# Pooled attention into a residual MLP on one core: a new order for the first batch, fillers on TensorE, and two transposes moved from DMA to TensorE in the second

## Chip, cores, metric

The kernel runs on one core of one Trainium2 chip. The metric is the time of one execution on the device in microseconds (us); the figure for a kernel is the median of its runs.

## What is computed

For each of 8 batches the reference does attention over 8 heads of 64 channels and 576 positions, with keys and values averaged over groups of 8 positions, so that a head has 72 keys. The heads side by side are the 512 channels of x. Then a mixer over positions and an MLP over channels follow, each with a residual.

```python
k_p = k.reshape(B, H, Sp, pool, D).mean(axis=3)      # pool = 8, Sp = 72; v_p likewise
attn = softmax(scale * np.matmul(q, k_p.transpose(0, 1, 3, 2)))
x = np.matmul(attn, v_p)                             # then (B, S, H * D)
a1 = alpha1 * x + beta1
tok = np.einsum('ts,bsd->btd', w_tok, a1)            # over the 576 positions
u = x + lam * tok
a2 = alpha2 * u + beta2
ch = np.maximum(a2 @ w_ch1, 0.0) @ w_ch2             # 512 -> 2048 -> 512
out = u + lam * ch
```

## The kernel before

Everything that TensorE multiplies is bf16 or fp16; sums are fp32 in PSUM. A batch has four chunks of 128 positions and a rest of 64; the rests of two batches share one chunk, so 8 batches make 36 chunks. Four chunks are one block of the MLP, and there are nine blocks.

**The stages of a batch.** `att_F` brings q to channel-major form (qT), `att_Frem` does so for the rest of 64 positions. `att_K` sums the keys in groups of 8 by a product with `pool_main` and evacuates them to `kpT`. `att_S` makes the scores of a head and ScalarE's exponential of them (ET, L441, two instructions a head). `first_V` (batches 0 and 1) pools the values by TensorE. `att_AV` multiplies by the values, and VectorE divides by the row sum into `x_tm` (L461, L463). `att_X` makes `xs`, the operand of the mixer, from two heads at a time (L470, L474), on VectorE or GpSimd. `mix_T` is the mixer of one chunk: five products (L504), then VectorE adds x (`u_sb`, L506) and scales to bf16 (`u_bf`, L508). `mix_uT` brings `u_bf` to channel-major form (`u_fm`), either by a DMA transpose on SyncE's queue (L518) or by four TensorE transposes (L523) and a ScalarE copy (L525).

**The MLP of a block.** `mlp_A(n, j)` is four products for 128 of the 2048 hidden channels and a ScalarE ReLU into Hj (L544). `mlp_B(n, m, part)` is four of the 16 products of one output chunk m (L557); after part 3, VectorE adds u (L562) and the result is stored. `scale_w2(g)` multiplies a quarter of the second weight by lam on VectorE (L327), once; `mlp_B` of block 0 takes its parts in the order of those quarters.

**What sets the order.** No scheduler moves anything: each engine runs its instructions in the order in which the code issues them, and waits only for semaphores. The first batch (L571 to L642) is written out call by call. From L690 on, each block n gathers a list of calls with a due number ("slot") and issues them sorted by it: `mlp_A` number j has slot j, the sixteen `mlp_B` have slots 16 to 31, and the attention of batch n + 1 is put between them by the numbers in `attention(b)`. Loads of batch n + 2 are in the same list. The numbers only order the calls; they are not times.

**Queues of DMAs.** SyncE issues q's rest, k and v from batch 2 on, the stores and the DMA transposes; GpSimd's queue issues all loads that change type (q, the first k and v, all weights), between its own arithmetic; ScalarE's queue issues the small vectors at the start. A load with `behind` is preceded by a one-column write of the destination on VectorE, so it can't start before VectorE has come to that place.

**Constants.** `broadcast` spreads a row over 128 partitions by an fp32 product with a row of ones (L266) and a ScalarE copy. `more_constants` (L252) makes ones, a zero tile `warm`, the zero rows of `xs` and `wtT`, and two products of one row each (L260). `setup_wtok` transposes the mixer's weight by TensorE, `setup_rowsum` makes its row sums, `setup_bias` the MLP's bias. `keep_warm(count)` (L490) is `count` products of 128 x 512 whose result nothing reads. `gp` (L52) takes one of six PSUM buffers.

Of the kernel before, what the change touches and what calls it, by code (L numbers as in the profile page):

```python
# [14 lines left out]
P = 128  # L15
# [8 lines left out]
def kernel(  # L24
# [102 lines left out]
    def load_v(b, u, parts=(0, 1)):  # L127

        if parts[0] == 0:
            st1[b]["v"][u] = work.tile([SPG, 4, 8, D], FP, tag="v_u", bufs=2, name="v_u")  # L130
        v_u = st1[b]["v"][u]
        for part in parts:
            g0, g1 = ((0, 64), (64, SPG))[part]
            nc.sync.dma_start(
                out=v_u[g0:g1].rearrange("g h p d -> g h (p d)"),
                in_=v[b, 4 * u:4 * u + 4, 8 * g0:8 * g1].rearrange("h (g p) d -> g h (p d)", p=8))
# [57 lines left out]
    load_vector(2, moe_alpha2)  # L194
    nc.scalar.dma_start(out=b2row, in_=moe_beta2.rearrange("(c p) -> c p", p=P))
    identity = const.tile([P, P], FP, tag="identity", name="identity")
# [14 lines left out]
    load_q_bf(0, 1)  # L211
    for t, n, width in ((pool_main, 64, 2),):
        nc.gpsimd.affine_select(out=t, in_=t, compare_op=ALU.is_ge, fill=0.0, base=0,
                                pattern=[[-width, n]], channel_multiplier=1)
        nc.gpsimd.affine_select(out=t, in_=t, compare_op=ALU.is_ge, fill=0.0, base=width - 1,
                                pattern=[[width, n]], channel_multiplier=-1)
# [4 lines left out]
    nc.gpsimd.affine_select(out=identity, in_=identity, compare_op=ALU.not_equal,  # L221
                            fill=1.0, base=0, pattern=[[-1, P]], channel_multiplier=1)
# [11 lines left out]
    for i in range(H):  # L234
# [3 lines left out]
    nc.vector.tensor_reduce(out=pool_rem, in_=pool_each, op=ALU.max, axis=AX.X)  # L238
# [5 lines left out]
                            in1=pool_v[0:32, 1:16:2], op=ALU.add)  # L244

    warm = const.tile([P, DM], BF, tag="warm", name="warm")
    b2c_bf = const.tile([P, 4], BF, tag="b2c_bf", name="b2c_bf")
    xs_pool = [const.tile([P, 5, DM], BF, tag=f"xs_{i}", name=f"xs_{i}") for i in range(2)]
# [3 lines left out]
    def more_constants():  # L252
        nc.vector.memset(ones_bf, 1.0)
        nc.vector.memset(ones_lo[0:64], 1.0)
        nc.vector.memset(ones_lo[64:128], 0.0)
        nc.vector.memset(warm, 0.0)
        nc.vector.memset(xs_pool[1][0:64, 4, :], 0.0)
        nc.vector.memset(wtT[:, :, S:640], 0.0)
        for i, p0 in ((0, 64), (1, 0)):
            nc.vector.tensor_tensor(out=xs_pool[i][p0:p0 + 1, 4, :], in0=vecs[p0:p0 + 1, 3],  # L260
                                    in1=vecs[p0:p0 + 1, 0], op=ALU.mult)
# [80 lines left out]
    def att_F(b, hp, copy=nc.scalar.copy):  # L342


        st = st1[b]
        u, r = hp // 2, hp % 2
        if r == 0:
            st["qT"][u] = work.tile([P, 8, P], BF, tag="qT", bufs=4, name="qT")
        if b:
            if r == 0:  # L350
                nc.sync.dma_start_transpose(out=st["qT"][u],
                                            in_=st["q"][u].rearrange("p h c d -> p (h c d)"))
            return
        ps_q = gp("ps_q").bitcast(BF)
        for c in range(4):
            nc.tensor.transpose(
                out=ps_q[:, 128 * c:128 * c + 128],
                in_=st["q"][u][:, 2 * r + c // 2, 2 * (c % 2):2 * (c % 2) + 2].rearrange(
                    "p c d -> p (c d)"),
                identity=identity_bf)  # L360
        copy(out=st["qT"][u][:, 4 * r:4 * r + 4, :],
                       in_=ps_q[:, 0:512].rearrange("p (c t) -> p c t", c=4))
# [16 lines left out]
    def att_K(b, u, copy):  # L379
# [13 lines left out]
        for hh in range(2):  # L393
            for c in range(nr):
                nc.tensor.matmul(  # L395
                    out=kp[:, hh:4:2, 64:72],
                    lhsT=st["rem"][1][:, hh, c:c + 2].rearrange("p a d -> p (a d)"),
                    rhs=pool_rem.rearrange("p (g u r) -> p u r g", r=2, u=2)[:, u],
                    start=(c == 0), stop=(c == nr - 1))
        for a in range(2):  # L400
# [89 lines left out]
    def keep_warm(count):  # L490

        ps = gp("ps_warm")
        for _ in range(count):
            nc.tensor.matmul(out=ps, lhsT=identity_bf, rhs=warm)
# [16 lines left out]
    def mix_uT(key):  # L511
# [5 lines left out]
        if key[0] > 1 or key in ((1, 0), (1, 1), (0, 4)):  # L517
# [53 lines left out]
    new_batch(1)  # L571
    broadcast(1, lamal_bc)
    broadcast(0, lam_bc)
    att_F(0, 0)
    att_F(0, 1, nc.vector.tensor_copy)
    cast_rem(0, nc.vector)
    att_K(0, 0, None)
    att_Frem(0, nc.scalar.copy)
    att_S(0, 0)
# [3 lines left out]
    att_S(0, 2)  # L583
    att_K(0, 1, None)
    nc.vector.tensor_tensor(out=lamal_bc, in0=lamal_bc, in1=lam_bc, op=ALU.mult)
    more_constants()
    att_S(0, 3)
    att_S(0, 4)
    first_V(0, 0)
    att_AV(0, 0)  # L590
    att_S(0, 5)
    att_AV(0, 1)
    for g in range(4):
        load_w1(g)
    att_X(0, 0, 2, nc.gpsimd)
# [5 lines left out]
    broadcast(2, al2_bc)  # L601
    setup_vectors()
    load_q_bf(1, 0)
    load_q_bf(1, 1)
    att_X(0, 2, 4, nc.gpsimd)
    load_w2(0)
# [3 lines left out]
    att_X(0, 4, 6)  # L610
# [5 lines left out]
    load_rem(1, behind=nc.vector)  # L616
# [4 lines left out]
    att_X(0, 6, 8)  # L621
    mix_T(0, 0, nc.gpsimd)
    setup_rowsum(2)
    setup_rowsum(3)
    mix_T(0, 1, nc.gpsimd)
    load_v16(1)
    for g in range(1, 4):
        load_w2(g)
# [16 lines left out]
    def attention(b):  # L645
# [4 lines left out]
        if first:  # L650
            todo.append((3.3, lambda: att_F(b, 0)))
            todo.append((3.4, lambda: att_F(b, 2)))
            todo.append((3.5, lambda: cast_rem(b, nc.gpsimd)))
            todo.append((6.0, lambda: att_Frem(b)))
# [10 lines left out]
        for u in range(2):  # L665
# [4 lines left out]
            if first:  # L670
                todo.append((10.2 + 1.4 * u, lambda u=u: first_V(b, u, nc.scalar.copy)))
        for h in range(8):
            at = 8.8 + 1.1 * h if first else 7.4 + 1.15 * h
            lag = 3.0 if first else 2.0
# [76 lines left out]
```

## Time and profile before

| what | us |
|---|---|
| median of three runs (lowest, highest) | 370.04 (369.24, 370.18) |
| the profiled execution's own time | 369.66 |
| its span, from the first instruction to the last | 368.0 |
| TensorE, products | 349.7 busy, 95% |
| VectorE | 213.3, 58% |
| ScalarE | 151.5, 41% |
| GpSimd | 89.2, 24% |
| mean granted clock of TensorE | 0.978 of full |

Times in the views count from the start of the span. A row of a timeline gives start, duration, engine, line and operation, what is written and read with its shape, how many instructions are merged, and in brackets the idle time before it and what ended that. A table by stretches gives the busy us of each engine in each stretch, the share of full clock that TensorE was granted, the mean busy share of the 16 DMA engines (over 1 where the packets of one engine overlap) and what they moved. Busy says that an engine had an instruction running, not that it ran at full speed.

### The profile page before, as it was taken

The page shows a single profiled execution, that of the slowest core. Times are in us where ns is not written, and L with a number is a line of the kernel's source. Part 1 is how long each engine was busy: PE and PEld are TensorE (multiplying, and loading weights), DVE is VectorE, ACT ScalarE, POOL GpSimd, SP SyncE. Part 2 cuts the span into 40 slices and gives each one's busy share as a digit, 9 for nine tenths or more (in the row PEclk, how much of TensorE's full clock was granted, in tenths as well). Part 3 has the DMA queues.
Part 4 walks back from the last instruction along what each step waited for, and adds up shares of the span by engine and source line. Part 5 has one row for each costly group of instructions (what it writes and reads, how often), then busy time and mean ns, then how long its engine had stood idle before and what let it go on. Part 6 is the DMA issues. An engine that isn't in the chain of part 4 may idle for free.

```text
span 368.0 us, 5803 instructions
## 1 busy us (share of the span) xinstructions
PE 349.7 (95%) x2161; PEld 190.7 (52%) x2201; DVE 213.3 (58%) x449; ACT 151.5 (41%) x312; POOL 89.2 (24%) x97
## 2 busy tenths in 40 slices
PE   5799899979999999999999999999999999999994
PEld 2566566435654565456545654565446544544542
DVE  5566035898777587658765887587748871011011
ACT  3434588014830483048303830384038403703700
POOL 8353905980004300250044003500330000000000
PEclk9958999999999999999999999999999999999998
DMA  8999994419829763688289728874730032011012
GB/s 127 203 205 256 187 272 93 58 35 235 161 73 219 141 126 68 175 179 159 72 209 145 139 74 207 149 143 83 206 89 0 20 96 71 2 57 57 3 57 57
DMA packets 69232, 45.17 MB, mean 123 GB/s; under 512 B 35850, under 2 KB 60494, under 8 KB 69204
## 3 DMA queue, kind: packets, MB, share of 16 engines
q1 hardware_dynamic: 54112, 34.03, 39.0%
q0 software_dynamic: 15072, 10.76, 19.9%
q8 instruction: 17, 0.28, 0.3%
q14 instruction: 11, 0.09, 0.1%
q10 hardware_dynamic: 20, 0.01, 0.0%
HBM read 38.04 MB, written 9.44 MB: 129 GB/s over the span
## 4 chain that ended last, share of the span: by engine, by line
PE 85%; DVE 6%; DMA 5%; issue 2%; ACT 1%; SPq 1%; DVEq 0%
PE ps_ch L557 32%; PE ps_h L539 31%; PE ps_tok L504 10%; PE ps_sc L436 4%; DMA v_u<-in_v_dram 3%; PE ps_av L455 2%; DMA rem_raw<-in_k_dram 1%; PE ps_sc L439 1%; DVE u_bf L508 1%; PE ps_kp L389 1%; DVE w L327 1%; DVE u_sb L506 1%; DVE x_tm L463 1%; DMA rem_qT<-rem_q 1%; DVE xs L470 1%
## 5 line engine op out<-in xcount | busy, mean ns | idle before, releaser
L544 ACT ACTIVATE Hj<-ps_h,bias_cols 128x512 bf16<-128x512 f32 x144 | 98.8, 688 | 158.6 <-PE ps_h L539 157.7
L539 PE MATMUL ps_h<-u_fm,w 128*128 128x512 bf16 (+2 forms) x572 | 137.1, 374 | 1.1
L557 PE MATMUL ps_ch<-w,Hj 128*128 128x512 bf16 x560 | 132.3, 379 | 0.9
L557 PEld LDWEIGHTS <-Hj 128*128 128x128 bf16 x576 | 55.0, 98 | 62.2
L539 PEld LDWEIGHTS <-w 128*128 128x128 bf16 x592 | 62.5, 114 | 44.8 <-issue 0.8
L562 DVE TENSOR_TENSOR u_sb<-u_sb,ps_ch 128x512 f32<-128x512 f32 x36 | 24.7, 687 | 75.5 <-PE ps_ch L557 75.2
L504 PE MATMUL ps_tok<-xs,wtT 128*128 128x512 bf16 (+1 forms) x197 | 49.5, 380 | 0.7 <-DVE xs L470 0.4
L441 ACT ACTIVATE ET<-ps_sc 72x256 f16<-72x256 f32 (+1 forms) x128 | 44.9, 405 | 6.7 <-PE ps_sc L436 6.3
L506 DVE TENSOR_TENSOR u_sb<-x_tm,ps_tok 128x512 f32<-128x512 f32 (+1 forms) x40 | 27.4, 686 | 26.4 <-PE ps_tok L504 26.4
L142 POOL CAST rem_q<-rem_raw 128x256 bf16<-128x256 f32 x7 | 5.3, 751 | 129.4 <-DMA rem_raw<-in_q_dram 129.3
L463 DVE TENSOR_TENSOR x_tm<-ps_av,rec 128x320 f32<-128x320 f32 x64 | 31.5, 492 | 2.3
L504 PEld LDWEIGHTS <-wtT 128*128 128x128 bf16 (+1 forms) x200 | 19.5, 98 | 24.3 <-issue 1.0
L508 DVE TENSOR_TENSOR u_bf<-u_sb,al_bc 128x512 bf16<-128x512 f32 (+1 forms) x38 | 29.4, 775 | 1.5
L461 DVE RECIPROCAL rec<-ps_av 128x5 f32<-128x5 f32 x64 | 12.3, 192 | 25.7 <-PE ps_av L459 24.8
L424 DVE TENSOR_TENSOR v_u<-v_u 72x512 f32<-72x512 f32 (+1 forms) x48 | 26.5, 553 | 1.2
L436 PE MATMUL ps_sc<-qT,kpT 128*72 128x256 bf16 x128 | 26.4, 288 | 0.7 <-ACT kpT L402 0.4
L455 PEld LDWEIGHTS <-ET 72*128 72x128 f16 x256 | 16.7, 102 | 14.7 <-DVE vp L417 2.9
L155 POOL TENSOR_TENSOR k_raw<-k_raw 128x512 f32<-128x512 f32 x14 | 18.7, 1333 | 14.6 <-DMA k_raw<-in_k_dram 11.3
L455 PE MATMUL ps_av<-vp,ET 72*128 72x66 f16 x256 | 19.1, 199 | 2.6 <-DVE vp L417 2.6
L157 POOL TENSOR_TENSOR k_bf<-k_raw 128x512 bf16<-128x512 f32 x14 | 21.3, 1524 | 1.1
L470 DVE TENSOR_TENSOR xs<-x_tm,lamal_bc 128x512 bf16<-128x512 f32 x27 | 18.7, 692 | 0.9
L402 DVE CAST kpT<-ps_kp 64x288 bf16<-64x288 f32 x26 | 11.8, 455 | 9.4 <-PE ps_kp L395 6.1
(109 smaller groups left out, 214.0 us busy)
## 6 DMA issues: line engine op xcount, KB each, us to landing
out_dram<-u_sb SPq DMA_DIRECT2D x32, 256.0 KB
k_raw<-in_k_dram SPq DMA_DIRECT2D x14, 512.0 KB
v_u<-in_v_dram SPq DMA_DIRECT2D x12, 512.0 KB
q_bf<-in_q_dram POOLq DMA_DIRECT2D x16, 256.0 KB, 5.0
w<-in_moe_w_ch_dram POOLq DMA_DIRECT2D x8, 512.0 KB, 11.1
rem_raw<-in_q_dram SPq DMA_DIRECT2D x16, 64.0 KB
rem_raw<-in_k_dram SPq DMA_DIRECT2D x16, 64.0 KB
v<-in_v_dram POOLq DMA_DIRECT2D x4, 256.0 KB, 6.1
```

The source lines that it names most:

```text
L424: nc.vector.tensor_tensor(out=t[:, :, 0:n], in0=t[:, :, 0:n], in1=t[:, :, n:2 * n], op=ALU.add)
L436: nc.tensor.matmul(out=ps_sc[0:SPG, 0:256], lhsT=kpT_pool[u][:, half, h % 4, :], rhs=st["qT"][u][:, 2 * (h % 4):2 * (h % 4) + 2, :])
L441: nc.scalar.activation(out=ET[:, n0:n0 + n], in_=ps_sc[0:SPG, 0:n], func=AF.Exp, bias=0.0, scale=0.125)
L455: nc.tensor.matmul(out=av[:, c, :], lhsT=ET[:, m0:m0 + 128], rhs=vp1[:, hh, :])
L463: nc.vector.tensor_tensor(out=x[:, :, dd:dd + D], in0=av[:, :, 0:64], in1=rec.unsqueeze(2).to_broadcast((P, 5, D)), op=ALU.mult)
L504: nc.tensor.matmul(out=ps_tok, lhsT=wtT[0:kk, at, t0:t0 + P], rhs=xs[0:kk, sc, :], start=(sc == 0), stop=(sc == 4))
L506: nc.vector.tensor_tensor(out=s["u"][p0:p1, :], in0=st1[b]["x"][p0:p1, c, :], in1=ps_tok[p0:p1, 0:DM], op=ALU.add)
L508: eng.tensor_tensor(out=s["u_bf"][p0:p1, :], in0=s["u"][p0:p1, :], in1=al2_bc[p0:p1, :], op=ALU.mult)
L539: nc.tensor.matmul(out=ps_h[:, t0:t1], lhsT=w1_of(cc, j), rhs=u_fm[n][:, cc, t0:t1], start=(cc == 0), stop=(cc == 3))
L544: nc.scalar.activation(out=t, in_=ps_h, func=AF.Relu, bias=bias_cols[:, j:j + 1], scale=1.0)
L557: nc.tensor.matmul(out=ps, lhsT=Hj[n, j][:, 128 * m:128 * m + 128], rhs=w2[j // 4][:, j % 4, :], start=(j == 0), stop=(j == NJ - 1))
L562: nc.vector.tensor_tensor(out=u, in0=u, in1=ps, op=ALU.add)
```

## The change

Five things are done.

- First batch, constants. `warm` and the zero rows of `xs_pool[1]` are made at the start. The two one-row products move from `more_constants` into `bias_rows`, called behind `cast_rem`. `more_constants`, with what is left of it, is called before the first scores instead of before the fourth. The product of `lamal_bc` and `lam_bc` runs inside the first `att_K`. `identity` is made earlier on GpSimd. `al2_bc` is no longer spread by TensorE: a DMA on SyncE loads it as a broadcast, behind a write of VectorE (`load_al2`). The transposed copy of q's second piece goes from VectorE to ScalarE, and `att_Frem` is before `att_K`.
- Unread products. `keep_warm` takes its PSUM from the pool of `ps_ch` and its weights from `warm`; nine products in seven more calls are put into the first batch.
- Order of loads and of `att_X` in the first batch: `load_w1(2)`, `load_w1(3)` and the four `load_w2` come later, batch 1's q, rest and v earlier, and the third `att_X` goes to GpSimd, so that its queue runs three `att_X` with no load between.
- Second batch. Its q (`att_F`, `att_Frem`) and its chunks 0 and 1 of u (`mix_uT`) are transposed by TensorE and copied by ScalarE, no longer by DMA.
- Slots in block 0: row sum 4 is parted from its transposes, `mix_T(0, 4)`, the scalings of w2, values, mixer and `mix_uT` of batch 1 move. `mix_uT` of chunk 3 goes from 26.8 to 29.1. The loads of batch 2's k, v and rest get a write of VectorE before them.

Core of the diff ("..." where lines are left out):

```diff
-    def load_v(b, u, parts=(0, 1)):
+    def load_v(b, u, parts=(0, 1), behind=None):
...
+        if behind is not None:
+            for rows_ in (slice(0, 64), slice(64, SPG)):
+                behind.memset(v_u[rows_, 0, 0, 0:1], 0.0)
...
-    load_vector(2, moe_alpha2)
...
+    warm = const.tile([P, DM], BF, tag="warm", name="warm")
+    nc.vector.memset(warm, 0.0)
...
+    nc.gpsimd.affine_select(out=identity, in_=identity, compare_op=ALU.not_equal,
+                            fill=1.0, base=0, pattern=[[-1, P]], channel_multiplier=1)
...
-    nc.gpsimd.affine_select(out=identity, in_=identity, compare_op=ALU.not_equal,
-                            fill=1.0, base=0, pattern=[[-1, P]], channel_multiplier=1)
...
-    nc.vector.tensor_reduce(out=pool_rem, in_=pool_each, op=ALU.max, axis=AX.X)
+    xs_pool = [const.tile([P, 5, DM], BF, tag=f"xs_{i}", name=f"xs_{i}") for i in range(2)]
+    nc.vector.memset(xs_pool[1][0:64, 4, :], 0.0)
...
+    nc.vector.tensor_reduce(out=pool_rem, in_=pool_each, op=ALU.max, axis=AX.X)
+
+    def bias_rows():
+        for i, p0 in ((0, 64), (1, 0)):
+            nc.vector.tensor_tensor(out=xs_pool[i][p0:p0 + 1, 4, :], in0=vecs[p0:p0 + 1, 3],
+                                    in1=vecs[p0:p0 + 1, 0], op=ALU.mult)
...
-    warm = const.tile([P, DM], BF, tag="warm", name="warm")
...
-    xs_pool = [const.tile([P, 5, DM], BF, tag=f"xs_{i}", name=f"xs_{i}") for i in range(2)]
...
-        nc.vector.memset(warm, 0.0)
-        nc.vector.memset(xs_pool[1][0:64, 4, :], 0.0)
...
-        for i, p0 in ((0, 64), (1, 0)):
-            nc.vector.tensor_tensor(out=xs_pool[i][p0:p0 + 1, 4, :], in0=vecs[p0:p0 + 1, 3],
-                                    in1=vecs[p0:p0 + 1, 0], op=ALU.mult)
+
+    def load_al2(behind):
+        behind.memset(al2_bc[:, 0:1], 0.0)
+        nc.sync.dma_start(out=al2_bc, in_=moe_alpha2.unsqueeze(0).to_broadcast((P, DM)))
...
-        if b:
+        if b > 1:
...
-    def att_K(b, u, copy):
+    def att_K(b, u, copy, between=None):
...
+        if between is not None:
+            between()
...
-        ps = gp("ps_warm")
+        ps = psB.tile([P, DM], FP, tag="ch", bufs=2, name="ps_warm")
...
-            nc.tensor.matmul(out=ps, lhsT=identity_bf, rhs=warm)
+            nc.tensor.matmul(out=ps, lhsT=warm[:, 0:P], rhs=warm)
...
-        if key[0] > 1 or key in ((1, 0), (1, 1), (0, 4)):
+        if key[0] > 1 or key == (0, 4):
...
+    keep_warm(2)
...
-    att_F(0, 0)
-    att_F(0, 1, nc.vector.tensor_copy)
+    keep_warm(1)
...
-    att_K(0, 0, None)
+    bias_rows()
+    att_F(0, 0)
+    att_F(0, 1)
...
+    keep_warm(1)
+    att_K(0, 0, None, lambda: nc.vector.tensor_tensor(out=lamal_bc, in0=lamal_bc, in1=lam_bc,
+                                                      op=ALU.mult))
+    more_constants()
+    keep_warm(2)
...
+    keep_warm(1)
...
-    nc.vector.tensor_tensor(out=lamal_bc, in0=lamal_bc, in1=lam_bc, op=ALU.mult)
-    more_constants()
+    load_al2(nc.vector)
...
+    setup_vectors()
+    keep_warm(1)
...
-    att_AV(0, 0)
...
+    att_AV(0, 0)
...
-    for g in range(4):
+    for g in range(2):
...
+    load_q_bf(1, 0)
+    load_q_bf(1, 1)
+    load_w1(2)
...
-    broadcast(2, al2_bc)
-    setup_vectors()
-    load_q_bf(1, 0)
-    load_q_bf(1, 1)
+    load_rem(1, behind=nc.vector)
...
-    load_w2(0)
...
-    att_X(0, 4, 6)
+    att_X(0, 4, 6, nc.gpsimd)
...
-    load_rem(1, behind=nc.vector)
...
-    mix_T(0, 0, nc.gpsimd)
...
+    load_v16(1)
+    keep_warm(1)
+    mix_T(0, 0, nc.gpsimd)
...
-    load_v16(1)
-    for g in range(1, 4):
+    load_w1(3)
+    for g in range(3):
...
-            todo.append((3.3, lambda: att_F(b, 0)))
-            todo.append((3.4, lambda: att_F(b, 2)))
+            for hp in range(4):
+                todo.append((2.6 + 0.9 * hp, lambda hp=hp: att_F(b, hp)))
...
-            todo.append((6.0, lambda: att_Frem(b)))
+            todo.append((3.65, lambda: load_w2(3)))
+            todo.append((7.4, lambda: att_Frem(b, nc.scalar.copy)))
...
-                todo.append((10.2 + 1.4 * u, lambda u=u: first_V(b, u, nc.scalar.copy)))
+                todo.append((11.0 + 1.2 * u, lambda u=u: first_V(b, u, nc.scalar.copy)))
...
-            lag = 3.0 if first else 2.0
+            lag = 3.3 if first else 2.0
...
-            at = 21.4 + 1.2 * c if first else 19.1 + 1.3 * c
+            at = 21.8 + 1.2 * c if first else 19.1 + 1.3 * c
...
+                if first and c in (2, 3):
+                    at += 1.3 * c - 2.0
+                elif first and c < 2:
+                    at += 1.0
...
-            todo.append((5.4, lambda: mix_T(0, 4)))
-            todo.append((4.6, lambda: (setup_wtok(4, nc.scalar.copy), setup_rowsum(4))))
-            todo.append((7.3, setup_wtok_odd))
+            todo.append((6.5, lambda: mix_T(0, 4)))
+            todo.append((4.6, lambda: setup_wtok(4, nc.scalar.copy)))
+            todo.append((6.2, lambda: setup_rowsum(4)))
+            todo.append((8.3, setup_wtok_odd))
...
-                todo.append(((8.0, 13.0, 20.3, 23.9)[g], lambda g=g: scale_w2(g)))
+                todo.append(((13.0, 16.6, 20.6, 24.4)[g], lambda g=g: scale_w2(g)))
...
+                gate = nc.vector if b == 1 else None
...
-                    at = 20.0 + 0.2 * u if b == 1 else 21.0 + 0.2 * u
-                    todo.append((at, lambda b=b, u=u: load_k(b + 1, u)))
+                    at = 21.0 + 0.2 * u
+                    todo.append((at, lambda b=b, u=u: load_k(b + 1, u, gate)))
...
-                    at = 22.0 + 0.2 * u if b == 1 else 3.5 + 4.0 * u
-                    todo.append((at, lambda b=b, u=u: load_v(b + 1, u)))
-                todo.append((20.1 if b == 1 else 20.9, lambda b=b: load_rem(b + 1)))
+                    at = 19.0 + 0.2 * u if b == 1 else 3.5 + 4.0 * u
+                    todo.append((at, lambda b=b, u=u: load_v(b + 1, u, behind=gate)))
+                todo.append((20.9, lambda b=b: load_rem(b + 1, behind=gate)))
```

More of the change, by code (lines that the diff above doesn't have):

```diff
@@ L571 @@
     new_batch(1)
+    keep_warm(2)
     broadcast(1, lamal_bc)
     broadcast(0, lam_bc)
+    keep_warm(1)
+    cast_rem(0, nc.vector)
+    bias_rows()
     att_F(0, 0)
-    att_F(0, 1, nc.vector.tensor_copy)
-    cast_rem(0, nc.vector)
-    att_K(0, 0, None)
+    att_F(0, 1)
     att_Frem(0, nc.scalar.copy)
+    keep_warm(1)
[3 more added lines that the diff above has]
+    keep_warm(2)
     att_S(0, 0)
@@ L583 @@
     att_S(0, 2)
+    keep_warm(1)
     att_K(0, 1, None)
-    nc.vector.tensor_tensor(out=lamal_bc, in0=lamal_bc, in1=lam_bc, op=ALU.mult)
-    more_constants()
+    load_al2(nc.vector)
     att_S(0, 3)
+    setup_vectors()
+    keep_warm(1)
     att_S(0, 4)
     first_V(0, 0)
+    att_S(0, 5)
     att_AV(0, 0)
-    att_S(0, 5)
     att_AV(0, 1)
-    for g in range(4):
+    for g in range(2):
         load_w1(g)
+    load_q_bf(1, 0)
+    load_q_bf(1, 1)
+    load_w1(2)
     att_X(0, 0, 2, nc.gpsimd)
@@ L621 @@
     att_X(0, 6, 8)
+    setup_rowsum(2)
+    load_v16(1)
+    keep_warm(1)
     mix_T(0, 0, nc.gpsimd)
-    setup_rowsum(2)
     setup_rowsum(3)
     mix_T(0, 1, nc.gpsimd)
-    load_v16(1)
-    for g in range(1, 4):
+    load_w1(3)
+    for g in range(3):
         load_w2(g)
```

## Prediction

> **What bounds the kernel now.** I read the page's busy lines first, then a table by stretches, then the timeline where that table shows gaps. The page says that TensorE is nearly always busy, and that its clock is low for a while near the start.
>
> ```profile
> PE 349.7 (95%) x2161; PEld 190.7 (52%) x2201; DVE 213.3 (58%) x449; ACT 151.5 (41%) x312; POOL 89.2 (24%) x97
> PE   5799899979999999999999999999999999999994
> PEclk9958999999999999999999999999999999999998
> DMA  8999994419829763688289728874730032011012
> ```
>
> The table by stretches (busy of TensorE, weight loads, VectorE, ScalarE, GpSimd; clock; DMA share; GB/s):
>
> ```profile
> 14.20:17.60 3.40, 1.94 (x18) 1.05 (x15) 2.56 (x9) 1.70 (x5) 0.00 (x0) 1.00 1.10 199
> 17.60:21.00 3.40, 1.91 (x17) 1.53 (x17) 2.85 (x8) 0.72 (x2) 0.00 (x0) 0.50 1.25 207
> 24.40:27.80 3.40, 3.40 (x36) 2.63 (x35) 1.80 (x5) 1.64 (x4) 2.19 (x3) 0.50 1.31 201
> 31.20:38.10 6.90, 6.83 (x60) 3.97 (x61) 4.06 (x6) 2.36 (x6) 4.92 (x6) 1.00 1.24 258
> 76.20:80.70 4.50, 2.18 (x14) 0.87 (x12) 4.43 (x4) 0.59 (x1) 4.42 (x3) 1.00 0.00 0
> 85.20:368.00 282.80, 276.23 (x1599) 145.92 (x1629) 163.75 (x334) 114.38 (x224) 39.19 (x38) 1.00 0.50 111
> ```
>
> Three regions follow. From 85.2 us (block 1's first product) TensorE is busy 276 of 283 us at full clock, and the change doesn't touch that work. Block 0 (38.1 to 85.2) is TensorE's too, with two holes. The first batch (0 to 38.1) has idle time and, from 17.6 to 31.2, half a clock, during which TensorE is solidly busy. So the end moves by what is won before 85.2. The timeline shows why:
>
> ```profile
> 6.21 1.03 PE L356 MATMUL ps_q<-identity_bf,q_bf 128*128 128x128 bf16 x8 [0.18 <-DMA q_bf<-in_q_dram]
> ...
> 17.32 1.39 DVE L260 TENSOR_TENSOR xs<-vecs 1x512 bf16<-1x512 f32 x2
> 18.75 0.48 DVE L417 CAST vp<-ps_v 72x128 f16<-72x128 f32 x2
> 19.09 0.40 PE L455 MATMUL ps_av<-vp,ET 72*128 72x66 f16 x4 [2.60 <-DVE vp L417]
> ...
> 35.64 0.39 PE L523 MATMUL ps_uT<-identity_bf,u_bf 128*128 128x128 bf16 x4
> ...
> 44.97 0.28 PE L296 MATMUL ps_rs<-wtT,ones_bf 128*128 128x64 bf16 x4 [1.31 <-ACT wtT L287]
> ...
> 75.59 3.35 DVE L327 TENSOR_TENSOR w<-w,lam_bc 128x2048 bf16<-128x2048 bf16 x1
> ...
> 80.67 0.40 PE L523 MATMUL ps_uT<-identity_bf,u_bf 128*128 128x128 bf16 x4 [2.32 <-DVE u_bf L508]
> ```
>
> VectorE makes constants from 15.3 to 18.7, so the pooled values (L417) are late and TensorE stands; then its clock halves. Eight transposes take 1.03 us at 6.2, four take 0.39 at 35.6: taking off a lone one's 0.31 and 0.22 us, 0.103 and 0.057 apiece. So the clock is half before 14.2 as well, where the table still prints 1.00. In block 0, TensorE waits 1.31 us for a ScalarE copy and 2.32 us for a `u_bf` that stands behind a weight scaling on VectorE.
>
> **What the skill says.** "TensorE: Matmul & The Clock Gate", Part 1, says that half the clock is the default and that a busy window of about 3.4 us releases it, an idle one takes it back. The trace agrees: full at 14.2, lost one window later (17.6), half for four windows, back at 31.2. The page's Part 4 says that transposes don't count as busy in the same way; that fits the half clock at 24.4 to 27.8 with TensorE busy 3.40 of 3.40 us on transposes and short products. "SBUF — State Buffer", Who interferes with whom, says that a VectorE instruction with two SBUF inputs blocks against a GpSimd one that reads: the scaling took 3.35 us beside GpSimd's key sums, and 2.27 alone at 48.7. "DMA: Bandwidth & Descriptors", Issuing engines are not separate DMA queues, says that all queues share 16 engines: the table's share is above 1 in 14 to 38 at about 205 GB/s, so a load that is moved forward pushes another back.
>
> **The change, part by part.** Times of before are in brackets.
>
> *Start to the first scores.* The two one-row products (2 x 0.68 = 1.37 us) now stand on VectorE behind the casts of the rest, which end at 8.69, and ahead of the copy of k for which `att_K` waits. That copy ends at 8.69 + 1.37 + 0.29 = 10.35 (8.9). Thirteen products (0.87), four of the rest (0.2), ScalarE's kpT copy (0.39) and VectorE's (0.46) give 12.2 (10.84), and two unread products of 0.43 us at half clock fit in that gap. First scores: 12.2 (10.40). This costs 1.8 us at that place.
>
> *To the last operand.* The exponentials take 0.72 us a head: eight, a kpT copy (0.39), the bias row (0.17) and some 0.6 of waiting for `att_K(0, 1)` bring ScalarE from 12.6 to 19.5 (23.7). VectorE has 0.7 us of constants at 12.2, long before `first_V`. With TensorE at full clock the values come at 17.4 to 17.9 and the first evacuation of `att_AV` starts at 18.4 (19.59). From there VectorE is the bound: 8 x 0.69 + 0.48 + 0.97 = 7.0 us, ending at 25.5 (30.34). The 10.75 us that this takes now come from TensorE at half clock and from `al2_bc`'s fp32 product (2.07 us, removed; its DMA, 0.26 MB issued at some 15 us, has 10 us to land). The three `att_X` on GpSimd (1.7 us each) end by 25.1. `mix_T(0, 0)`: 25.5 (30.29), so **4.8 us** won.
>
> *To block 0.* From there to 38.10 took 7.8 us; the first mixer (1.54 for 1.08) and a row sum get 0.7 shorter. Block 0 starts at 32.6: **5.5 us** won.
>
> *Unread products.* They lie in waits. Where no wait covers one it costs 0.43 us at half clock and 0.22 at full; nine bare ones would be 1.9 to 3.9 us. I take zero, keeping 1 us in the range. Whether they hold the clock is not shown by the trace: from 10.8 to 14.2 dense work brought it, and 1.94 us of short products in 14.2 to 17.6 lost it. Adding up streamed columns times the used part of the array, I estimate a third to two fifths of full activity per window in the new order, against a sixth in the window that lost it. I take "held from about 13 us".
>
> *Loads.* Moved loads land in time if 205 GB/s holds: w1(2) ends 4.7 MB (the page's sizes, summed) at about 27 us; batch 1's k (issued at 24.5, sharing with it) at about 34, GpSimd's sums end near 40, and `att_K(1, 0)` comes at 42. w1(3) and w2 follow at about 38 to 48, needed from 49 on. No cost.
>
> *Second batch on TensorE.* 16 + 2 + 8 transposes x 0.055 = **+1.4 us** on TensorE. ScalarE gets four copies of 0.59, one of 0.36 and two of 0.59. Before 58 us it was busy 14.1 of 20 us from 38 on, and gets 2.7 more, just where ReLUs are queued; the six PSUM buffers cover most. I take +0.6 us of waiting, bounds 0 and 2.7. What is removed from SyncE's queue (five DMA transposes) was waited for by no one.
>
> *Slots.* Parting row sum 4 from its copy removes 1.31 us. `mix_uT` of chunk 3 at 29.1 has three more groups of `mlp_B` ahead (2.6 us), which removes 2.32 if the scalings come in time. All four now stand in VectorE's busy stretch: from the first `att_AV` 8 x 0.69 + 2 x 2.3 + 0.97 = 11.1 us, where TensorE needs about 11.5; then one scaling, three chunks of 1.4, the last scaling: 8.8 us more. That ends about 78.7 on the old clock of the block, and `mlp_B` needs it at about 79.2. So it just fits; bounds 0 and 2 us.
>
> **Sum.** Block 0: 1.4 + 0.6 - 1.31 - 2.32 = -1.6. Start: -5.5. Together -7.1 from the profiled execution's 369.66 us (span 368.0 and 1.66 around it): 362.6; the median of the runs is 0.4 above that execution, so I put **362.8**.
>
> **Rivals.**
> - *The clock stays at half* from the first `att_AV` to the mixer. For it: short products and transposes didn't raise it in 17.6 to 27.8. Against: the fillers, and one idle stretch less. TensorE then needs 11.2 - 2.1 (`al2_bc`) + 1.0 (third row sum, filler) = 10.1 us from 19.3, so the mixer starts at 29.4, and 1.6 us are won in all; with block 0, 369.7 - 3.2 + 0.2 = **366.7**.
> - *Batch 2's k comes late* (slower). Its load now waits for VectorE behind the third scaling, about 72 on the old clock, with v and q of batch 2 ahead: 3.0 MB from 66 on, at 205 GB/s landed at 80.7. GpSimd then needs 6.9 us of casts and sums, and `att_K(2, 1)` comes at 89.4: 1.8 us to spare. Each us past 82.5 is one of TensorE's. At 115 GB/s it lands at 92.1, 9.6 us late: **372.4**. It decides from a landing at 89.7 on (7.2 us late), some 127 GB/s. Against it: slices of over 200 GB/s are on the page wherever loads are queued.
> - *Block 0 takes the gain back*: ScalarE's 2.7 and the scalings' 2 us at their upper bounds make block 0 1.4 + 2.7 + 2 - 3.6 = 2.5 us longer, and bare fillers cost 3.0: 5.5 - 5.5, **369.9**.
> - *VectorE isn't delayed at the start* (the rest comes earlier than the 8.2 us at which it lands now, or the first copy finds room): 1.8 us more, and the 0.6 of waiting for ScalarE nil: **360.4**.
>
> **Chances.** Forecast (360.5 to 364.6) 0.58; half clock 0.20; late k 0.09; taken back 0.06; more 0.07 (358.5 to 361). The range 359.5 to 367.5 holds the first two, but for the half clock's end at 368, and half of the last: 0.8. About 0.3%, 1.1 us, is what a measurement of this kernel can tell from no change: faster 0.85, same 0.06, slower 0.09.
>
> **What would show it.** Right: full clock in the stretches from about 14 us on; the first L504 product near 25.5 and block 0's first L539 near 32.6; no idle over 1 us before L296 and L523 in block 0; the first L436 at about 12. Wrong: 0.50 between 18 and 28; idle of `att_K` for k_bf in block 1; idle of L557 or L523 behind L327; ScalarE full and L539 waiting for it from 40 to 57.

## The result

The changed kernel takes 371.39 us (median of 4 runs, 371.05 to 371.80); the kernel before took 369.87 beside it (4 runs, 369.24 to 370.18). The ratio is 1.0044, with a 95% interval of 1.0027 to 1.0061: a little slower. The forecast was 362.8 us with a range up to 367.5, so it is 8.6 us off and has the wrong sign.

The profiled execution of the changed kernel took 371.48 us (span 369.8), 1.82 more than that of the kernel before (369.66).

### The profile page after: what moved, and what is told of

The parts are those of the page before. It is cut to its first block, busy times and chain, and to the rows that moved or that the text cites. A ratio compares the mean times of both kernels' runs of the same rounds, so it can differ in the third digit from the quotient of the medians.

```text
span 369.8 us, 5920 instructions
## 1 busy us (share of the span) xinstructions
PE 353.8 (96%) x2234; PEld 190.1 (51%) x2234; DVE 213.2 (58%) x454; ACT 154.5 (42%) x319; POOL 87.7 (24%) x99
## 4 chain that ended last, share of the span: by engine, by line
PE 87%; DVE 4%; DMA 3%; ACT 3%; SPq 1%; issue 1%; DVEq 0%; ACTq 0%
PE ps_ch L567 32%; PE ps_h L549 32%; PE ps_tok L514 12%; PE ps_sc L446 4%; DMA rem_qT<-rem_q 2%; PE ps_av L465 2%; ACT Hj L554 2%; DVE x_tm L473 1%; DMA rem_raw<-in_k_dram 1%; PE ps_sc L449 1%; PE ps_kp L397 1%; PE ps_warm L504 1%; DVE w L335 1%; SPq L122 1%; SPq L359 1%
## 5 line engine op out<-in xcount | busy, mean ns | idle before, releaser
L549 PE MATMUL ps_h<-u_fm,w 128*128 128x512 bf16 (+2 forms) x592 | 140.1, 378 | 0.3 <-ACT ET L451 0.2
L567 PE MATMUL ps_ch<-w,Hj 128*128 128x512 bf16 x576 | 134.2, 379 | 0.0
L549 PEld LDWEIGHTS <-w 128*128 128x128 bf16 x592 | 63.0, 114 | 50.3 <-issue 6.9
L145 POOL CAST rem_q<-rem_raw 128x256 bf16<-128x256 f32 x7 | 3.0, 430 | 136.7 <-DMA rem_raw<-in_q_dram 136.7
L471 DVE RECIPROCAL rec<-ps_av 128x5 f32<-128x5 f32 x64 | 12.2, 191 | 30.2 <-PE ps_av L469 29.4
L434 DVE TENSOR_TENSOR v_u<-v_u 72x512 f32<-72x512 f32 (+1 forms) x48 | 27.9, 581 | 1.2
L160 POOL TENSOR_TENSOR k_bf<-k_raw 128x512 bf16<-128x512 f32 x14 | 19.8, 1411 | 1.1
L449 PE MATMUL ps_sc<-rem_qT,kpT 128*72 128x64 bf16 x64 | 15.8, 246 | 4.3 <-DMA rem_qT<-rem_q 4.3
L465 PE MATMUL ps_av<-vp,ET 72*128 72x66 f16 x256 | 18.2, 194 | 0.3 <-ACT wtT L295 0.3
```

The lines of the kernel that those rows point to most:

```text
L434: nc.vector.tensor_tensor(out=t[:, :, 0:n], in0=t[:, :, 0:n], in1=t[:, :, n:2 * n], op=ALU.add)
L465: nc.tensor.matmul(out=av[:, c, :], lhsT=ET[:, m0:m0 + 128], rhs=vp1[:, hh, :])
L549: nc.tensor.matmul(out=ps_h[:, t0:t1], lhsT=w1_of(cc, j), rhs=u_fm[n][:, cc, t0:t1], start=(cc == 0), stop=(cc == 3))
L567: nc.tensor.matmul(out=ps, lhsT=Hj[n, j][:, 128 * m:128 * m + 128], rhs=w2[j // 4][:, j % 4, :], start=(j == 0), stop=(j == NJ - 1))
```

## The profile after

From the page of the changed kernel: the busy line, and the rows of TensorE, its granted clock and the DMA share in 40 slices (9.2 us each).

```profile
PE 353.8 (96%) x2234; PEld 190.1 (51%) x2234; DVE 213.2 (58%) x454; ACT 154.5 (42%) x319; POOL 87.7 (24%) x99
...
PE   7889999995999999999999999999999999999994
...
PEclk9999999999799999999999999999999999999998
DMA  8999900979907872778368838785730042011012
```

The low clock at the start is gone. In its place there is a TensorE slice of 5 (the tenth) and a clock of 7 in the eleventh, at 83 to 101 us: a place where the change moves none of TensorE's work, with a DMA share of 9 beside it. The table by stretches (columns as in the prediction's table) shows the first batch and then that place:

```profile
18.00:21.00 3.00, 2.99 (x39) 2.05 (x38) 2.37 (x10) 1.54 (x5) 0.56 (x1) 1.00 1.25 218
21.00:24.00 3.00, 2.65 (x52) 2.31 (x49) 2.86 (x11) 2.37 (x6) 3.00 (x5) 1.00 1.24 213
...
87.00:90.00 3.00, 0.52 (x4) 0.26 (x3) 2.65 (x7) 0.95 (x2) 0.00 (x0) 1.00 1.34 183
90.00:93.00 3.00, 1.22 (x4) 0.48 (x4) 0.00 (x0) 0.43 (x1) 0.00 (x0) 0.64 1.13 209
93.00:96.00 3.00, 3.00 (x14) 1.48 (x13) 0.00 (x0) 1.30 (x4) 0.00 (x0) 0.50 1.05 183
96.00:99.00 3.00, 3.00 (x22) 1.80 (x20) 1.36 (x4) 2.12 (x6) 0.00 (x0) 0.73 1.25 143
```

From 18 to 24 us TensorE has full clock, where it had half. From 87 to 93 us it is busy 1.7 of 6 us, and then its clock is at half. The lost part of the clock in the last three rows, (0.36 + 0.50 + 0.27) x 3, is 3.4 us, which is 6.8 us at half. The timeline of the changed kernel gives the milestones and the wait:

```profile
12.26 0.75 PE L446 MATMUL ps_sc<-qT,kpT 128*72 128x256 bf16 x2
25.71 1.24 PE L514 MATMUL ps_tok<-xs,wtT 128*128 128x512 bf16 x5 [0.67 <-DVE xs L480]
32.78 0.81 PE L549 MATMUL ps_h<-u_fm,w 128*128 128x384 bf16 x4
...
42.87 0.39 PE L514 MATMUL ps_tok<-xs,wtT 65*128 65x512 bf16 x1 [0.55 <-ACT wtT L306]
64.94 1.25 PE L514 MATMUL ps_tok<-xs,wtT 128*128 128x512 bf16 x5 [1.10 <-DVE xs L480]
...
79.87 4.48 PE L549 MATMUL ps_h<-u_fm,w 128*128 128x512 bf16 x20
81.70 2.84 SPq L359 DMA_TRANSPOSE qT<-q_bf  x2
82.85 1.53 POOL L77 DMA_DIRECT2D q_bf<-in_q_dram  x2
84.64 1.72 SPq L377 DMA_TRANSPOSE rem_qT<-rem_q  x1
...
91.78 0.24 PE L449 MATMUL ps_sc<-rem_qT,kpT 128*72 128x64 bf16 x1 [4.27 <-DMA rem_qT<-rem_q]
```

Block 1 (first L549 at 79.87, in the kernel before at 85.22) starts 5.35 us early. From there to the end of the execution it is 371.48 - 79.87 = 291.61 us, where the kernel before took 369.66 - 85.22 = 284.44: 7.17 us are lost behind block 1's start. 4.27 of them are one wait of TensorE, in the first head's scores of batch 2, for the DMA transpose of the rest of q, and the remaining 2.9 are laid to the half clock that comes with it; experiment 3 tests that.

In the kernel before the same three DMAs stand in another order:

```profile
80.00 1.54 POOL L77 DMA_DIRECT2D q_bf<-in_q_dram  x2
...
86.92 3.46 SPq L351 DMA_TRANSPOSE qT<-q_bf  x2
90.48 1.19 SPq L369 DMA_TRANSPOSE rem_qT<-rem_q  x1
```

There batch 3's q load (L77, GpSimd's queue) is issued 6.9 us ahead of the transposes of batch 2's q; after the change it is issued 1.2 us behind the first of them. That the load moved has a chain of causes. The gates (`gate = nc.vector`) hold batch 2's k back until VectorE has written its destination. So GpSimd's key sums of batch 2, the last of which is L160, end at 82.9, with block 1 (and so the transposes) now starting 5.35 us sooner; the q load stands behind those sums on GpSimd. From 86 to 90 us load and transposes share the 16 DMA engines, and the rest's transpose lands 7.1 us after its issue, where it took 2.5.

These 7.1 us are mostly waiting behind another transpose. SyncE's three land in the order of their issue, at 85.18, 91.38 and 91.74 us. Between 86 and 90 us some 920 of their packets pass beside the load, of 256 bytes each; the second transpose of q (256 KB) has 1,024 of them, the rest (64 KB) 256. So it is above all the second transpose of q that the load slows: it lands 8.3 us after its issue, where it took 4.2. The rest lands 0.36 us behind it, as before the change (0.27).

## Experiments

Two theories stood against each other. **A**: the q load beside the transposes makes them late, and the wait with the half clock behind it is the whole loss. **B**: the transposes are late by their own place in SyncE's queue (stores and transposes ahead of them), and the load has nothing to do with it. All kernels are the changed one with the edit shown, unless another base is named. Beside these runs the kernel before spread more widely than in the result, so the ratios have wide intervals. The changed kernel was not measured again beside them, and the medians of the kernel before are 370.35 to 371.26 there, where it was 369.87: a difference from 371.39 can be off by about 1 us.

**1. No gates.** `e1_ungated`:

```diff
-                gate = nc.vector if b == 1 else None
+                gate = None
```

> The loads of batch 2's rest, k and v lose the write of VectorE ahead of them; all else is the changed kernel. Theory A (collision): the gates make GpSimd's key sums of batch 2 late (they end at 82.9 us), so batch 3's q load, next in GpSimd's queue, runs at 84 to 90 us beside the DMA transposes of batch 2, the last of which lands 4.3 us late; then TensorE's clock halves for 6.8 us, worth 3.4. Without gates the sums end early, q is loaded before the transposes: 371.4 - 4.3 - 3.4 = 363.7 us, up to 1.5 more where GpSimd and VectorE now meet in block 0. Theory B (queue order): the last transpose is late since it stands third in SyncE's queue behind the stores of block 0; the gates don't matter: 371.4 within 1 us.

Measured: 366.54 us (364.94 to 367.91), ratio 0.9867 (0.9802 to 0.9933). GpSimd's sums end early, the q load is issued at 75.95, and of the 4.27 us these waits are left:

```profile
87.46 0.38 PE L446 MATMUL ps_sc<-qT,kpT 128*72 128x256 bf16 x2 [1.10 <-DMA qT<-q_bf]
88.85 0.24 PE L449 MATMUL ps_sc<-rem_qT,kpT 128*72 128x64 bf16 x1 [1.01 <-DMA rem_qT<-rem_q]
```

Freed of the gates, GpSimd's sums meet VectorE again, though: its last scaling of w2 takes 3.35 us, as in the kernel before, where the gated kernel's four take 2.28 to 2.33. The clock is at half for 3.41 us from 89.67 on. In the two of the four runs that kept full clock (0.999 and 1.0) the time is 364.94 and 365.70 us. So the gates do something; what they cost is the load behind them.

**2. The q load first, the gates kept.** `e2_q3_early` issues batch 3's q load right behind batch 2's q load:

```diff
-                    todo.append((at if b == 1 else 0.4 + 0.1 * u,
-                                 lambda b=b, u=u: load_q_bf(b + 1, u)))
+                    if b != 2:
+                        todo.append((at if b == 1 else 0.4 + 0.1 * u,
+                                     lambda b=b, u=u: load_q_bf(b + 1, u)))
+                    if b == 1:
+                        todo.append((21.5 + 0.1 * u, lambda b=b, u=u: load_q_bf(b + 2, u)))
```

> Only batch 3's q load moves: it is issued by GpSimd right behind batch 2's q load, ahead of the key sums of batch 2. Theory A: no q load beside the transposes, idle of L449 in block 1 below 0.5 us, clock full there: 363.7 us; the 0.5 MB ahead of batch 2's k may delay the key sums by 2 to 2.5 us, which may cost up to 1 us. Theory B: 371.4 within 1 us.

Measured: 365.85 us (365.80 to 365.88), ratio 0.985 (0.9794 to 0.9906). SyncE's queue is as before this edit (qT issued at 82.05, the rest at 85.27), only the load is away, and the wait for the rest is gone. One wait remains, because k's load now stands behind the q load and the key sums start at 79.22, not 76.88:

```profile
89.96 0.30 PE L446 MATMUL ps_sc<-qT,kpT 128*72 128x256 bf16 x1 [1.10 <-DVE kpT L412]
```

B as it was put falls: the order in SyncE's queue is the same, and the transposes are in time. But A includes the queue: the load slows the second transpose of q, and the rest is late because it stands behind that one.

**3. The wait filled.** `e3_filled_wait` leaves the collision and puts twenty unread products where TensorE waits:

```diff
             todo.append((0.2, lambda: att_Frem(b)))
+            todo.append((7.39, lambda: keep_warm(20)))
```

> The changed kernel with 20 unread products (20 x 0.216 = 4.3 us at full clock) ahead of batch 2's first scores, where TensorE waits 4.3 us. The transfer is as late as before. If the half clock behind the wait is a cost of its own, as both theories have it (6.8 us at half, 3.4 us lost): 368.0 us. If what runs at half clock there is hidden behind ScalarE or a transfer: 371.4.

Measured: 368.89 us (368.07 to 369.93, 20 runs), ratio 0.9942 (0.9918 to 0.9966).

```profile
86.73 4.48 PE L504 MATMUL ps_warm<-warm 128*128 128x512 bf16 x20
```

The rest is as late as before, but the mean granted clock is 1.0, not 0.987. So some 2.5 us of the loss are the clock's, and what is left is the wait's.

**4. The rest first in SyncE's queue.** `e4_rest_first`:

```diff
-            todo.append((0.2, lambda: att_Frem(b)))
+            todo.append((-1.2, lambda: att_Frem(b)))
```

> Only the order of three DMA transposes in SyncE's queue changes: that of batch 2's rest goes ahead of the two of its q. Both theories: the rest's transpose lands before the first scores, no idle there, 363.7 us; by theory A the second q transpose still takes 4 us beside the q load, but it is not needed before about 92 us. If the time stays at 371, the wait for that transpose only stands in for another one behind it.

Measured: 367.59 us (364.98 to 370.03), ratio 0.9896 (0.982 to 0.9972). The wait has moved to the next transpose in the queue:

```profile
87.78 0.38 PE L446 MATMUL ps_sc<-qT,kpT 128*72 128x256 bf16 x2 [1.21 <-DMA qT<-q_bf]
```

The rest, now first, lands 2.5 us after its issue. The first transpose of q has moved back beside the load and lands 5.4 us after its own (82.26 to 87.64), where in the changed kernel it took 3.5. The four runs spread over 5 us. The profiled one is the fastest, with a mean clock of 0.998; the slowest has 0.987, so part of the spread is the clock. What it waited for was not seen.

**5. Both repairs.** `f1_both` is e2 with

```diff
-                gate = nc.vector if b == 1 else None
+                gate = None
```

> Both repairs at once: no VectorE writes before batch 2's loads of k, v and rest, and batch 3's q load issued early. With the early q load alone, 1.1 us of TensorE's wait was left before batch 2's third score, because the key sums ended late. If those sums are late only because the k loads are held back, this wait goes: no idle above 0.5 us in 80 to 95 us, full clock, 364.8 us (365.9 less 1.1). If the remaining wait has another cause (VectorE's value sums, which stand ahead of the copy of the keys), it stays: 365.9. If the freed loads collide with the transposes again: 366.5 or more.

Measured: 365.38 us (364.89 to 365.56), ratio 0.9859 (0.9816 to 0.9902). The wait for the keys goes, as expected, but another takes its place:

```profile
88.24 0.24 PE L449 MATMUL ps_sc<-rem_qT,kpT 128*72 128x64 bf16 x1 [1.25 <-DMA rem_qT<-rem_q]
```

The q load isn't beside it this time: the rest is issued at 85.86 and lands 2.4 us later, its undisturbed time. It is its place in SyncE's queue that is late, behind stores whose sums VectorE makes late, as it again has a scaling of 3.35 us. Here, then, B's mechanism is real, with 1.25 us and not 4.27.

**6. Without the nine fillers.** `f2_nofill` is e2 without the seven calls of `keep_warm` that the change added to the first batch:

```diff
-    keep_warm(2)
     broadcast(1, lamal_bc)
     broadcast(0, lam_bc)
-    keep_warm(1)
     cast_rem(0, nc.vector)
...
-    keep_warm(1)
     mix_T(0, 0, nc.gpsimd)
```

> The kernel with the early q load, without the nine unread products of the first batch. If these hold the clock, it is half in the stretch from about 17 to 27 us, the first mixer product comes 3 to 4 us later (29 against 25.7), and the time is 369 to 370. If the moved constants alone keep TensorE dense enough, the clock stays full and the time is 365.9 within 0.6.

Measured: 366.13 us (365.76 to 366.95), ratio 0.9884 (0.9846 to 0.9922). By stretches:

```profile
18.00:21.00 3.00, 3.00 (x36) 2.02 (x35) 1.75 (x7) 1.50 (x5) 0.00 (x0) 1.00 1.24 206
21.00:24.00 3.00, 2.64 (x52) 2.22 (x49) 2.86 (x13) 2.50 (x7) 2.90 (x4) 1.00 1.31 236
24.00:27.00 3.00, 1.94 (x22) 1.31 (x21) 2.60 (x8) 2.05 (x5) 3.00 (x5) 1.00 1.30 205
```

The clock is full there without them. The clock record begins with full clock at 17.96 us, in the kernels that have the fillers at 13.3 to 17.3, so they may bring it a little earlier; one profile doesn't show that. From the first scores to the first mixer product it is 26.37 - 12.70 = 13.67 us, with the fillers 25.68 - 12.07 = 13.61. The medians differ by 0.28 us, which these runs don't tell from nothing.

**7. The second batch's transposes back on DMA.** `f3_dma_turn` is e2 with

```diff
-        if b > 1:
+        if b:
...
-            todo.append((7.4, lambda: att_Frem(b, nc.scalar.copy)))
+            todo.append((7.4, lambda: att_Frem(b)))
...
-        if key[0] > 1 or key == (0, 4):
+        if key[0] > 1 or key in ((1, 0), (1, 1), (0, 4)):
```

> The kernel with the early q load, with the second batch's q, its rest and chunks 0 and 1 of u transposed by DMA again as before the change. If the turn over TensorE is a plain cost of the 2.0 us by which TensorE's busy time in block 0 grew, with the forecast's wait on ScalarE on top, this is 363.3 to 363.9. If the DMA transposes come late beside the weights' loads, which the change moved into the same stretch, TensorE waits in 40 to 50 us for them and the time is 366 or more.

Measured: 386.71 us (383.03 to 387.27), ratio 1.0415 (1.0354 to 1.0477).

```profile
62.31 0.24 PE L449 MATMUL ps_sc<-rem_qT,kpT 128*72 128x64 bf16 x1 [16.85 <-DMA rem_qT<-rem_q]
...
100.06 7.42 PE L549 MATMUL ps_h<-u_fm,w 128*128 128x512 bf16 x20 [3.47 <-DMA u_fm<-u_bf]
```

It is the same collision, four times as large: the DMA transposes of batch 1's q and rest are issued from 26.7 to 37.6 us, in the stretch into which the change moved the loads of v and of the weights, and the rest, behind the two of q, is ready only at 62.3, when the last of w2 has landed. In the kernel before, q's were through at about 40 us, before those loads; only the rest's ran beside them (issued at 39.9, its packets last to about 48) and nobody waited for it.

**8. Two scalings earlier.** `f4_scale_early` is e2 with

```diff
-                todo.append(((13.0, 16.6, 20.6, 24.4)[g], lambda g=g: scale_w2(g)))
+                todo.append(((9.5, 12.0, 20.6, 24.4)[g], lambda g=g: scale_w2(g)))
```

> The kernel with the early q load, with the first two scalings of the second weight moved from slots 13.0 and 16.6 to 9.5 and 12.0, where VectorE is idle for 7.9 us. If TensorE's 1.1 us wait for the mixer's operand in block 0 comes from the scalings in VectorE's busy stretch (the forecast's 'just fits'), it goes and the time is 364.8. If VectorE's own chain of evacuations sets it, it stays: 365.9.

Measured: 364.62 us (363.82 to 365.29), ratio 0.9839 (0.9799 to 0.9879). The wait before the mixer is gone; block 0 takes 77.68 - 31.79 = 45.89 us, with e2's slots 79.81 - 32.75 = 47.06.

**9. The rest on TensorE, on top of that.** `g1_rest_te` is f4 with

```diff
-            todo.append((0.2, lambda: att_Frem(b)))
+            todo.append((0.2, lambda: att_Frem(b, nc.scalar.copy)))
```

> The kernel with the early q load and the early scalings (364.6 us, with waits of 0.54 us for rem_qT and 0.45 us for the keys left in block 1), and batch 2's rest of q transposed by TensorE and copied by ScalarE. If the DMA transpose of the rest is what is late, the 0.54 us wait goes and 0.1 us of products comes: 364.2, with the 0.45 us for the keys left. If ScalarE's copy stands behind ReLUs for too long, a wait for ACT takes its place: 364.6 or more.

Measured: 363.74 us (363.51 to 364.67), ratio 0.9786 (0.9724 to 0.9848). No wait for `rem_qT` remains; the one for the keys is 1.15 us in this profile.

**10. The same one edit on the changed kernel.** `g2_after_rest_te` is the changed kernel with

```diff
-            todo.append((0.2, lambda: att_Frem(b)))
+            todo.append((0.2, lambda: att_Frem(b, nc.scalar.copy)))
```

> The changed kernel with one edit: batch 2's rest of q is transposed by TensorE and copied by ScalarE; the q load of batch 3 stays where the change put it and still runs beside the DMA transposes of q. If the whole loss of the changed kernel is the one wait for rem_qT and the half clock behind it (4.3 + 3.4 us), this is 363.7 to 365.5, at full clock. If the two large DMA transposes are just as late beside that load, TensorE waits for qT instead, some 2 to 4 us, and the time is 367 to 371.

Measured: 364.06 us (363.58 to 365.55), ratio 0.9796 (0.9732 to 0.9861). The stretches of the loss now read:

```profile
87.00:90.00 3.00, 3.00 (x25) 1.96 (x23) 2.69 (x7) 2.65 (x8) 0.00 (x0) 1.00 1.54 153
90.00:93.00 3.00, 3.00 (x27) 1.90 (x26) 2.33 (x7) 2.92 (x7) 0.00 (x0) 1.00 1.27 190
```

Six of six us, at full clock. One small transpose moved to TensorE gives back 371.39 - 364.06 = 7.3 us, close to the 7.17 of the accounting above. The large transposes run beside the load as before, but what they bring is needed later.

**11. The one-row products elsewhere.** `g3_bias_late` is g1 with `bias_rows` between the second key products and their copies, where VectorE is idle:

```diff
-    bias_rows()
     att_F(0, 0)
...
-    att_K(0, 1, None)
+    att_K(0, 1, None, bias_rows)
```

> The kernel before it in this call, with the two one-row products moved from in front of the first key copy into the second key product, where VectorE is idle for 1.7 us. If they are what delays the start, as the forecast costed (1.4 us of VectorE ahead of the copy), the first scores and the first mixer product come 1.4 us earlier and the time is 1.4 us lower: 362.8. If the exponentials or the values' load set the first batch, nothing is won: 364.2.

Measured: 362.14 us (361.81 to 363.40), ratio 0.9744 (0.9681 to 0.9807), 1.6 us under g1, beside which it was measured.

```profile
9.47 0.88 PE L397 MATMUL ps_kp<-pool_main,k 128*128 128x64 bf16 x13 [0.60 <-DVE k L394]
```

TensorE's wait for the copy of the first keys is 0.60 us, where it is 2.17 in the changed kernel and 1.95 in g1. This is the fastest version found, under both kernels.

**12. The fillers alone, in the kernel before.** `g4_before_fill` is the kernel before with the zero tile made early and the nine unread products added:

```diff
     new_batch(1)
+    keep_warm(2)
     broadcast(1, lamal_bc)
     broadcast(0, lam_bc)
+    keep_warm(1)
...
+    keep_warm(1)
     mix_T(0, 0, nc.gpsimd)
```

> The kernel before, with nothing but the nine unread products in the places where the change has them (and the zero tile for them made early). If they alone hold the clock, it is full from 18 to 31 us, the first mixer product comes some 3 us earlier than 30.29, and the time is 3 us under that of the kernel before: ratio 0.992. If the clock is lost because TensorE stands while VectorE makes constants, nine products don't change that: ratio 1.000 to 1.003.

Measured: 369.93 us (368.57 to 374.52, 20 runs), ratio 0.9972 (0.994 to 1.0003).

```profile
18.00:21.00 3.00, 1.80 (x20) 1.23 (x21) 2.56 (x8) 0.70 (x2) 0.00 (x0) 0.89 1.24 207
21.00:24.00 3.00, 3.00 (x18) 2.12 (x19) 1.86 (x6) 1.44 (x4) 3.00 (x4) 0.50 1.25 207
24.00:27.00 3.00, 3.00 (x35) 2.38 (x34) 1.77 (x5) 1.60 (x4) 2.42 (x4) 0.50 1.28 203
```

VectorE still makes constants when the pooled values are due, TensorE still stands (1.80 of 3.00 us), and the clock is lost. It goes at 20.37 us for 10.24 us, where it went at 17.60 for 13.65, and the first mixer product comes at 29.52 (30.29).

## Why the prediction was wrong

**The start: right.** The first scores came at 12.26 (forecast 12.2), the first mixer product at 25.71 (25.5), block 0 at 32.78 (32.6): 5.32 us won of 5.5. Between them two errors cancel: the first evacuation of `att_AV` came at 19.01 (18.4), and VectorE's work from there to the last operand took 6.55 us (7.0). Experiment 11 shows the price put on the one-row products (1.37 us) to be real: moving them gave 1.6.

**The clock: right, but not for the reason given first.** It held from 15.72 us on (forecast: about 13), where the clock record begins with full clock. The forecast counted the fillers for it; experiments 6 and 12 show that they are neither needed nor enough. What is left of the change, the moved constants and the order of the first batch, holds it; which part of that does was not tried.

**Block 0: right mechanisms, a term too small.** 1.6 us were forecast, 47.12 - 47.09 = 0.03 came. The two old waits went (1.31 + 2.32), the transposes cost what was said (26 x 0.055 = 1.43; four take TensorE 0.22, from 77.92 to the next product at 78.14), ScalarE's waits are 0.55 + 0.23 for a forecast 0.6. What failed is "So it just fits" for VectorE: the scalings among its evacuations delay the mixer's operand, and TensorE waits 1.10 us. Experiment 8 moves two scalings into VectorE's idle time, and 1.17 come back. 3.63 - 1.43 - 1.88 leaves 0.32 where 0.03 was measured; the 0.29 is not assigned.

**Behind block 0: the step that failed.** It is the line of the first part that the change doesn't touch the work from block 1 on, "So the end moves by what is won before 85.2", with "No cost" under *Loads*. They put everything behind block 0 at nothing; 7.17 us were lost there. The forecast followed each moved load to its own landing. It didn't ask what is queued behind the last of them on GpSimd, nor what runs on the DMA engines when that one lands. The rival *Batch 2's k comes late* looked at the right place with the wrong victim: the keys were ready in time, `att_K(2, 1)` at 86.09 waited for nothing. What was late were the transposes of q in SyncE's queue, down to the small one of the rest at its end, because the q load that follows the key sums had slid from 6.9 us ahead of them to just behind the first.

That slide has two parts, and both came from what the forecast did see: the gates make the key sums end at 82.9 (80.0 before), and the 5.35 us won bring the transposes forward by as much. A gain ahead of a transfer that doesn't come forward with it can itself bring two transfers together. Experiments 1, 2 and 10 take away the cause, the load and the victim in turn, and each gives back 4.9 to 7.3 us; with the victim gone the kernel takes 364.06 us. The sum with only this step mended is 369.66 - 5.32 - 0.03 = 364.3. (The prediction's own sum has a slip that doesn't bear on this: 362.6 and 0.4 are 363.0, not 362.8.)

**The half clock: an amount that no rival had.** The forecast priced late data at one us per us. With the wait of 4.27 us came 6.83 us at half clock, from 90.81 on, and 2.5 us (experiment 3) to 2.9 us more. The prediction quotes from the Trainium skill, "TensorE: Matmul & The Clock Gate", Part 1, that an idle window of about 3.4 us takes the clock back; this wait is longer than one, and that could have told it. But a wait needn't be so long: in experiment 1 waits of 1.10 and 1.01 us close together brought 3.41 us at half clock, in experiment 12 waits of 1.30 and 2.33 us did so too, and in the kernel before the same two waits (1.31 and 2.32) did not. How much clock is lost also differs between executions of one kernel: those of the kernel before beside the experiments took 368.8 to 369.3 us at a mean clock of 0.986 and 373.0 to 374.1 at 0.969 to 0.970. The four windows at half clock that the forecast started from are those of one execution.

**The turn over TensorE: its worth was not seen.** The forecast booked it at +1.4 us for nothing removed, since no one waited for the DMA transposes in the kernel before. Experiment 7 shows that with the loads in their new order they would have cost 386.71 - 365.85, some 21 us. It was a condition for the other moves.

## What to carry to other kernels

When transfers are moved, list for each stretch what shares the DMA engines in it, and look first at DMA transposes whose result TensorE needs soon, with what stands ahead of them in their queue. A small one at the end of such a queue cost next to nothing on TensorE here (experiment 10). Follow a moved load through the queue of the engine that consumes it to the next DMA which that engine issues. Don't price a wait on TensorE at its length alone: the clock can come on top, here 2.5 to 2.9 us for a wait of 4.27.

## What the runs showed of the hardware

**DMA transposes beside loads.** The transposes go by packets of 256 bytes, and the packet records of the trace tell how they share. Alone, in the kernel before, they pass at up to 1,120 per us (91 to 92 us). In the changed kernel, beside the q load with its packets of 512 bytes, it is 240 to 290 per us, with 220 to 235 of the load (87 to 90 us). In experiment 7, beside w2's packets of 4,096 bytes, it is a mean of 51 per us, with 38 of the load (48 to 60 us). That is 1.0 to 1.4 packets of the transpose for one of the load, so with the longer packets of the load the transpose was slower. The Trainium skill, "DMA: Bandwidth & Descriptors", Queues, rings and completion order, says that a DMA engine takes turns between its queues a packet at a time; these counts fit that, though the runs don't show whether a record of the trace is a packet in the page's sense. So the time of a DMA transpose depends on what runs beside it and on what is ahead of it in its queue. From issue to landing, the second transpose of q (256 KB) took 4.2 us in the kernel before, 8.3 in the changed one and 29.5 in experiment 7. The 64 KB of the rest took 2.5, 7.1 and 26.5 us there, nearly all of it behind that transpose; with the transposes ahead of it landed 0.4 us after its issue, but loads of v and the weights beside it, it took 9.6 (the kernel before, batch 1, issued at 39.85).

**The clock.** Each stretch at half clock lasted 3.41 us or a whole multiple (3.41, 6.83, 10.24, 13.65, 17.07), apart from the one in which a trace ends. The prediction's estimate of activity, streamed columns times the used part of the array, can be worked out for every stretch of 3.41 us in all fourteen traces, from the grant of full clock on; full activity is then a product of 512 columns on the whole array every 0.216 us, as in experiment 3. By this estimate, full clock was kept after all 1,390 stretches with at least 0.35 of full activity and lost after all 19 with at most 0.25; of seven between, three lost it. The lowest that kept it among the 1,390 is in the kernel without fillers (from 17.96 us), so that one holds the clock by a small margin. From half clock it came back after eight of nine stretches with at least 0.39, and after none of ten with less. The wait of 4.27 us fills one stretch, with 0.00. Some records of products are missing from the traces, so these limits are rough.
